# Turning the rows of every expert block on VectorE, from quarters of 64 columns

## The chip, the cores and the metric

The kernel runs on one core of a Trainium2 chip. The metric is device time in microseconds (us), the median of several runs. The engines are named as in the profile: PE is TensorE (PEld its weight loads), DVE is VectorE, ACT is ScalarE, POOL is GpSimd, and SP is SyncE, which here only issues DMAs.

## The reference

A Fourier mixing step over eight batches of 2496 rows with 256 columns is followed by a mixture of eight experts, in which each row goes to the one expert with the largest logit:

```python
X = np.fft.fft(np.fft.fft(x, axis=1), axis=2).real      # (8, 2496, 256)
x = X.reshape(19968, 256)
logits = x @ w_gate                                      # 8 experts
e = argmax(logits);  gate = softmax(logits)[e]
out = gate * (relu(x @ w1[e]) @ w2[e])                   # w1: 256 x 1024, w2: 1024 x 256
```

All of it is in float32.

## The kernel before

**Stages.** For each batch `b` there are three. `first(b)` and `regroup(b)` do one part of the transform along the rows and pass it through a DRAM tensor `Td`. `second(b)` ends the transform, finds each row's expert (`route`), and puts the row with POOL's indirect DMAs into a DRAM tensor `Xs`, which has a region for each expert. `experts` then takes blocks of 512, 256 or 128 rows of one expert from `Xs`, multiplies them with that expert's weights, and scatters the results to `out`.

**Order.** The order on each engine is written out by hand: the generators of the stages are advanced against each other by the loop over batches at line 956, with `AHEAD` (12) early steps of the next batch. Each engine works through its own instructions in program order, and so does SP's queue of DMA issues.

**Blocks.** `in_order` lists 66 blocks. Numbers 0 and 1 have 256 rows, 2 to 5 have 128, 6 to 9 have 256, 10 to 37 have 512 (10 to 12 come from batch 2). Then, in the last stage, seven blocks of 256 rows are woven with 21 blocks of 128 rows. The last seven of these 21 are computed only if the count in `tabs["cnt"]` reaches them; with the inputs here, the last three are skipped by PE, while their rows and weights are still loaded.

**Two kinds of block.** `halved(b, size)` tells them apart. Halved blocks (512 rows from batch 3 on, and the 256-row blocks of the last batch) use seven products instead of eight (`seven`, and in the last batch also `lower`), for which DVE first forms sums of the weights (`Left`, line 570) and of the rows (`right`, lines 575 to 578). All other blocks (0 to 12 and the 21 of 128 rows) use plain products: `ph` (the first layer, line 805), then `py` (the second, line 846).

**Rows of a block.** `fetch_rows` loads the rows, `turn` makes `xT` of them, with columns on the partitions and the odd columns negated. In a halved block the rows come in four DMAs of 64 columns each (L539), with the row number and gate in a fifth (L543); DVE's 32x32 transpose reads them (L588), and ACT negates one half (L590). In the other blocks one DMA brings whole rows (L534); PE transposes them against the identity into PSUM (`pt`, L596), and DVE evicts with signs (L597).

**Order of loads.** `fetch_some` issues the rows and then the weights (`w1` at L549, `w2` at L551) of a block up to two ahead, as buffers come free: `xb`, `w1` and `w2` have three each, `xT` has one. The next block is turned while the present one is at its second layer. Other transfers on SP's queue are the loads of `x` (L292), the writes and reads of `Td` (L345, L357).

Of the kernel before, what the change touches and what calls it, by code (L numbers as in the profile page):

```python
# [12 lines left out]
F32 = mybir.dt.float32  # L13
BF16 = mybir.dt.bfloat16
I32 = mybir.dt.int32
ALU = mybir.AluOpType
ACTF = mybir.ActivationFunctionType
# [3 lines left out]
B, S, D = 8, 2496, 256  # L21
# [16 lines left out]
BIG, BLK, REST = 512, 256, 128  # L38
# [8 lines left out]
def free(ap, offset, *dims):  # L47
    return bass.AP(ap.tensor, ap.offset + offset, [list(ap.ap[0])] + [list(d) for d in dims])


def bc(ap, axis, n):
    shape = list(ap.shape)
    shape.insert(axis, n)
    return ap[tuple([slice(None)] * axis + [None])].to_broadcast(shape)


def shape_consts():

    c = {}
    n1 = np.arange(NA)[:, None]  # L60
    r = np.arange(NP)
    k1 = r // 2
    im = r % 2

    def wave(n2, f):
        return f(2 * np.pi / S * ((NB * n1 + n2) * k1 % S))

    w1 = [np.where(im, wave(n2, np.sin), wave(n2, np.cos)) for n2 in range(1, NS)]
    for f in (np.cos, np.sin):
        w1 += [np.where(im, 0.0, wave(0, f)), np.where(im, wave(NS, f), 0.0)]  # L70
    c["w1"] = np.stack(w1, 1) * (k1 < NK)

    u, cs, s = np.meshgrid(np.arange(NU), np.arange(2), np.arange(NS), indexing="ij")
    u, cs, s = (v.reshape(-1, 1) for v in (u, cs, s))
    k2 = np.arange(NB)
    t = 2 * np.pi / NB * ((s + 1) * k2 % NB)
    end = np.where(cs, 1.0 - 2.0 * (k2 % 2), 1.0)
    even = np.where(s == NS - 1, end, np.where(cs, -np.sin(t), np.cos(t)))
    odd = np.where(s == NS - 1, end, np.where(cs, np.cos(t), np.sin(t)))
    own = (u == np.arange(NU)).astype(float)  # L80
    c["m2"] = np.stack([(own[:, :, None] * m[:, None, :]).reshape(GP, GP) for m in (even, odd)], 1)

    rot = np.zeros((GP, GP))
    for p in range(GP):
        if p % NS == NS - 1:
            rot[p, p] = 1.0
        elif p // NS % 2:
            rot[p, p - NS] = -1.0
        else:
            rot[p, p + NS] = 1.0  # L90
    c["rot"] = rot

    d = np.arange(H)[:, None]
    m = np.arange(D + 1)
    t = 2 * np.pi / D * (d * m % D)
    rc, rs = np.cos(t), -np.sin(t)
    rs[0] = 1.0 - 2.0 * (m % 2)
    full = np.concatenate([rc[:, :D], rs[:, :D]], 0)


    rd = np.zeros((H, 2, 2 * E + NY + 1))
    sign = 1.0 - 2.0 * (m[:NY] % 2)
    rd[:, 0, 0:NY] = sign * rc[:, 0:NY]
    rs[0] = 0.0
    rd[0, 1, 2 * E] = 1.0
    rd[:, 1, 2 * E + 1:] = sign * rs[:, 0:NY]
    c["rd"] = rd
    c["alt"] = np.broadcast_to(np.array([1.0, -1.0]), (128, 2))
    c["rt"] = full.T.reshape(2, 128, D).transpose(1, 0, 2)

    p = np.arange(128)[:, None, None, None]
    h = np.arange(2)[None, :, None, None]
    g = np.arange(HW)[None, None, :, None]
    mir = np.arange(2)
    tau = 128 * (HW * h + g) + p
    k1 = tau // NB
    k = k1 + NA * (tau % NB)
    bad = (k1 >= NK) | ((mir == 1) & ((k1 == 0) | (k1 == NK - 1)))
    row = np.where(bad, 0, np.where(mir, S - k, k))
    c["row"] = row.reshape(128, 2, NSL)  # L120
    c["good"] = 1.0 - bad.reshape(128, 2, NSL)
    c["far"] = OUT * bad.reshape(128, 2, NSL)
    c["rev"] = np.broadcast_to(E - np.arange(E), (128, E))
    c["cap"] = np.broadcast_to(CAP * np.arange(E), (128, E))
    c["sgn"] = np.where(np.arange(128) == 0, 1.0, -1.0)[:, None]
    c["lane"] = np.arange(128)[:, None]
    c["tri"] = np.triu(np.ones((128, 128)), 1)
    c["ident"] = np.eye(128)
    return {n: np.ascontiguousarray(v, dtype=np.float32) for n, v in c.items()}


# [61 lines left out]
def halved(b, size):  # L193

    return size == 512 and b > 2 or size == 256 and b == B - 1
# [22 lines left out]
def kernel(ctx: ExitStack, tc, x, w_gate, w1, w2, out):  # L218
    nc = tc.nc
    vec, act, pool = nc.vector, nc.scalar, nc.gpsimd  # L220
# [5 lines left out]
    Xs = nc.dram_tensor("Xs", (ROWS, W), F32, kind="Internal").ap()  # L226

    def const_dram(name, v):
        return nc.inline_tensor(v, name=f"c_{name}").ap()
# [17 lines left out]
    def taken(ins, b):  # L247
        ins = getattr(ins, "ins", ins)
        if b + 1 < B:
            tc.declare_no_dep(ins, group=f"xs{b + 1}", reason="a block has rows of its round's batches alone")  # L250
        tc.add_to_no_dep_group("taken", ins)
# [7 lines left out]
    pse = ctx.enter_context(tc.tile_pool(name="pse", bufs=1, space=PSUM))  # L259
# [4 lines left out]

    ctx.enter_context(tc.manual_schedule())
    consts = shape_consts()

    side = [n for n in consts if n not in ("w1", "rt")]
    packed = np.zeros((128, sum(consts[n][0].size for n in side)), np.float32)
    table = cp.tile(list(packed.shape), F32, name="table")  # L270
    con, k = {}, 0
# [9 lines left out]
    wg = cp.tile([128, 2, E], F32, name="wg")  # L281
    tri = cp.tile([128, 128], BF16, name="tri16")
    ones = cp.tile([128, 128], BF16, name="ones16")
    ident = con["ident"]
    waves = const_dram("w1", consts["w1"])

    def load(b, q):
# [239 lines left out]
    def fetch_rows(b, size, tab, i):  # L527


        n = size // 128  # L530
        row = nc.sync.value_load(tab[:, 0, i:i + 1], min_val=0, max_val=ROWS - size)
        xb = bp.tile([128, BIG // 128, W], F32, tag="xb", name="xb", bufs=3)
        if not halved(b, size):
            taken(nc.sync.dma_start(out=xb[:, 0:n].rearrange("p t c -> p (t c)"),  # L534
                                    in_=Xs[ds(row, size)].rearrange("(p t) c -> p (t c)", t=n)), b)
            return xb, xb[:, 0:n, D:]
        flat = xb[:].rearrange("p t c -> p (t c)")
        for q in range(4):
            taken(nc.sync.dma_start(  # L539
                out=flat[32 * q:32 * q + 32, 0:2 * size].rearrange("p (j e) -> p j e", e=64),  # L540
                in_=Xs[ds(row, size), 64 * q:64 * q + 64].rearrange("(j k) e -> k j e", k=32)), b)
        meta = flat[:, 4 * D:4 * D + 2 * n].rearrange("p (t c) -> p t c", c=2)
        taken(nc.sync.dma_start(out=meta, in_=Xs[ds(row, size), D:].rearrange("(t p) c -> p t c", p=128)), b)  # L543
        return flat, meta
# [27 lines left out]
    def right(xs, b11, b12, b21, b22, eng=vec):  # L572

        o = [xs[:, k] for k in range(3)]
        eng.tensor_tensor(o[0], b12, b11, op=sub)
        eng.tensor_tensor(o[1], b22, o[0], op=sub)
        eng.tensor_tensor(o[2], b21, o[1], op=sub)
        eng.tensor_tensor(b12, b22, b12, op=sub)
        return b11, b21, b22, o[2], o[0], o[1], b12

    def turn(b, size, xb):


        xT = bp.tile([128, 2, BIG], F32, tag="xT", name="xT", bufs=1)
        n = min(size // 128, 2)
        for h in range(-(-size // 256)):
            if halved(b, size):
                vec.transpose(free(xT[:], 256 * h, [32, 8], [BIG, 2], [1, 32]),  # L588
                              free(xb, 512 * h, [64, 8], [1, 2], [2, 32]))
                act.activation(xT[:, 1, 256 * h:256 * h + 256], xT[:, 1, 256 * h:256 * h + 256], ACTF.Copy, scale=-1.0)  # L590
                yield xT
                continue
            pt = pse.tile([128, 2, n, 128], F32, tag="e", name="pt")
            for c in range(2):
                for t in range(n):
                    nc.tensor.transpose(pt[:, c, t], xb[:, 2 * h + t, c:D:2], ident[:])  # L596
            vec.tensor_tensor(xT[:, :, 256 * h:256 * h + 128 * n], pt[:].rearrange("p c t k -> p c (t k)"),  # L597
                              bc(con["alt"][:], 2, 128 * n), op=ALU.mult)
            yield xT
        if halved(b, size):  # L600
            th = size // 2
            xs = bp.tile([128, 3, th], F32, tag="xs", name="xs", bufs=1)
            r = right(xs, *(xT[:, c, k * th:(k + 1) * th] for c in range(2) for k in range(2)))
            yield r
# [109 lines left out]
    def experts(todo):  # L714
# [35 lines left out]
        for k, (b, size, last, at) in enumerate(todo):  # L750
            n, m = size // 128, BIG // size
            if not k:
                while todo[0][:3] not in tabs:
                    yield 0, False
                fetch_some(0, 1)
                while b not in whole:
                    yield 0, True
                fetch_some(0)
                for _ in range(9):
                    yield 0, False  # L760
                for xT in turn(b, size, xbs[0][0]):
                    pass
# [163 lines left out]
    for _ in first(0):  # L926
# [8 lines left out]
        out=Xs[E * CAP:].rearrange("(k p) w -> p k w", k=BLK // 128), in_=bc(pad[:], 1, BLK // 128)), "xs"), 0)  # L935
# [103 lines left out]
```

## Time and profile before

| | |
|---|---|
| median of 4 runs | 1299.88 us (1297.93 to 1300.76) |
| profiled execution | 1302.36 us, of which span 1300.6 us |
| PE transposes `pt` (L596) | 98, median 281 ns, their busy time together 18.3 us |
| DVE evictions of `pt` (L597) | 37 (25 of 256 columns, mean 417 ns; 12 of 512, mean 686 ns) |
| DVE transposes (L588) | 57 of 512 columns, mean 692 ns |
| ACT negations (L590) | 57 of 256 columns, mean 415 ns |
| row loads in one DMA (L534) | 34 |
| row loads in quarters (L539) | 128, that is 32 blocks, and 32 of L543 |
| granted clock of PE, mean | 0.976 |

The profile is of one execution on the chip. Its page gives the busy time of each engine and, in 40 slices, the course of it; groups of instructions by line; and the chain of work that ended last. Timelines give each instruction with its start, duration, line, operation and tiles, and in brackets how long its engine was idle before it and what ended that. Durations of matmuls are modelled and overlap, so what an instruction costs PE is better read from the distance between starts. A DMA issue on SP shows the time of issuing, not of the transfer. Nearly all matmuls are issued by one helper and so stand under L223; they are told apart by their tiles.

### The profile page before, as it was taken

Reading aid. Unit: us, or ns where it says so; the run is one execution under the profiler, and the core shown is the slowest. Engines: PE = TensorE matmul, PEld = TensorE weight load, DVE = VectorE, ACT = ScalarE, POOL = GpSimd, SP = SyncE. Lnnn points to the kernel's source line nnn. Section 1 sums busy time; section 2 is a strip of 40 time slices with the busy share of each in tenths; the row PEclk is TensorE's granted clock in tenths of the full one; section 3 lists DMA queues with packets and bytes.
Section 4 is the critical chain, followed back from the end, with each engine's and each line's share of the span. In section 5 each row is a group of like instructions: output and inputs, shape, how many; then the busy total and the mean of one; then the engine's idle time right before and its main releaser. Section 6 shows DMA issues by size and latency. Waiting matters only on the chain.

```text
span 1300.6 us, 20743 instructions
## 1 busy us (share of the span) xinstructions
PE 1238.7 (95%) x7003; PEld 1092.1 (84%) x7003; DVE 700.6 (54%) x1772; ACT 424.1 (33%) x1059; POOL 361.5 (28%) x355
## 2 busy tenths in 40 slices
PE   6669898999999999999999999999989999999997
PEld 4558797876788888888888888888889999999996
DVE  4455434333456555666546455675468784444662
ACT  1423222331334343434334343432234332222231
POOL 0244216125014311351114411351344221111112
PEclk9859899999999999999999999999999999999998
DMA  8778697556446444583335534453345237777776
GB/s 240 251 239 281 230 325 273 200 174 229 136 134 215 162 145 154 145 263 118 113 117 181 158 104 159 125 168 106 117 126 172 90 107 287 265 279 286 276 298 234
DMA packets 134024, 249.76 MB, mean 192 GB/s; under 512 B 85065, under 2 KB 99891, under 8 KB 114332
## 3 DMA queue, kind: packets, MB, share of 16 engines
q1 hardware_dynamic: 117143, 203.33, 48.1%
q0 software_dynamic: 15888, 42.14, 9.0%
q10 hardware_dynamic: 885, 2.94, 0.7%
q8 instruction: 57, 0.93, 0.3%
q14 instruction: 51, 0.42, 0.1%
HBM read 194.97 MB, written 54.83 MB: 192 GB/s over the span
## 4 chain that ended last, share of the span: by engine, by line
PE 72%; issue 18%; POOL 3%; DMA 3%; DVE 2%; another core or an unknown queue 1%; ACT 1%; POOLq 0%; SPq 0%; ACTq 0%; DVEq 0%
PE py L223 29%; PE a L223 8%; PE c L223 7%; PE ph L223 7%; PE p L223 6%; PE d L223 4%; PE b L223 4%; PE e L223 3%; PE s L223 3%; POOL out_dram L238 3%; DMA xq<-in_x_dram 1%; DMA Td<-t 1%; PE pt L596 0%; DMA t<-Td 0%
## 5 line engine op out<-in xcount | busy, mean ns | idle before, releaser
L223 PE MATMUL py<-w_sb,hT 128*128 128x256 f32 x2016 | 457.0, 381 | 5.8 <-issue 5.8
L223 PEld LDWEIGHTS py<-w_sb,hT 128*128 128x128 f32 x2016 | 378.4, 191 | 55.3 <-issue 6.7
L238 POOL DMA_INDIRECT out_dram<-y,ro x163 | 163.2, 1001 | 731.2 <-ACT y L850 493.3
L238 POOL DMA_INDIRECT Xs<-rows,pi x160 | 163.0, 1019 | 200.0 <-ACT pi L470 82.8
L223 PE MATMUL ph<-xT,w_sb 128*128 128x128 f32 (+2 forms) x992 | 171.9, 329 | 6.5 <-DVE hT L809 5.6
L850 ACT ACTIVATE y<-py,xb 128x256 f32<-128x256 f32 x129 | 61.2, 474 | 325.8 <-PE py L223 285.3
L223 PEld LDWEIGHTS ph<-xT,w_sb 128*128 128x128 f32 x992 | 136.1, 192 | 31.1 <-issue 16.3
L223 PE MATMUL a<-xT,w_sb 128*128 128x256 f32 (+1 forms) x512 | 118.0, 357 | 3.0 <-ACT hT L644 2.0
L634 DVE TENSOR_TENSOR u<-p,b 128x512 f32<-128x512 f32 x57 | 39.2, 687 | 126.6 <-PE b L223 90.8
L809 DVE TENSOR_SCALAR hT<-ph 128x512 f32<-128x512 f32 x43 | 29.7, 691 | 138.0 <-issue 70.7
L223 PEld LDWEIGHTS a<-xT,w_sb 128*128 128x128 f32 x512 | 89.2, 190 | 15.0 <-ACT hT L644 3.6
L411 DVE COPY lg<-p 128x16 f32<-128x16 f32 x80 | 13.9, 174 | 144.9 <-ACT zs L408 139.0
L644 ACT ACTIVATE hT<-a 128x512 f32<-128x512 f32 x57 | 34.0, 597 | 156.7 <-PE a L223 120.4
L223 PE MATMUL s<-xq,w 104*112 104x256 f32 (+2 forms) x208 | 62.4, 424 | 13.0 <-DVE xq L300 11.0
L223 PEld LDWEIGHTS p<-table,t 120*128 120x128 f32 x352 | 54.6, 204 | 16.2 <-issue 5.3
L223 PE MATMUL p<-table,zz 128*128 128x145 f32 (+1 forms) x320 | 58.5, 309 | 6.6 <-issue 2.9
L223 PE MATMUL p<-table,t 120*128 120x120 f32 (+1 forms) x352 | 57.6, 290 | 7.0 <-ACT zz L382 3.3
L223 PE MATMUL c<-xT,ws 128*128 128x256 f32 (+1 forms) x256 | 59.2, 358 | 3.0 <-DVE hT L640 3.0
L811 ACT ACTIVATE hT<-ph 128x512 f32<-128x512 f32 x55 | 32.8, 597 | 83.0 <-PE ph L223 57.1
L223 PEld LDWEIGHTS s<-xq,w 104*112 104x112 f32 x208 | 39.4, 206 | 23.1 <-DVE xq L300 10.2
L223 PE MATMUL c<-xs,ws 128*128 128x256 f32 (+1 forms) x256 | 58.8, 357 | 0.0
L223 PE MATMUL d<-xT,w_sb 128*128 128x256 f32 (+1 forms) x256 | 58.7, 356 | 0.0
(148 smaller groups left out, 1761.5 us busy)
## 6 DMA issues: line engine op xcount, KB each, us to landing
w_sb<-in_moe_w_dram SPq DMA_DIRECT2D x132, 1024.0 KB
xq<-in_x_dram SPq DMA_DIRECT2D x24, 896.0 KB
xb<-Xs SPq DMA_DIRECT2D x100, 128.0 KB
Td<-t SPq DMA_DIRECT2D x18, 448.0 KB
t<-Td SPq DMA_DIRECT2D x8, 768.0 KB
t<-Td SPq DMA_DIRECT2D x8, 640.0 KB
xb<-Xs SPq DMA_DIRECT2D x25, 129.0 KB
Td<-t ACTq DMA_DIRECT2D x6, 448.0 KB
```

Source lines behind the costliest of these rows:

```text
L223: nc.tensor.matmul(o, lhsT=lhsT, rhs=rhs, start=start, stop=stop, **kw)
L238: return unordered(pool.indirect_dma_start(out=dst, out_offset=bass.IndirectOffsetOnAxis(ap=idx, axis=0), in_=rows, in_offset=None, bounds ...
L411: vec.tensor_copy(lg[:, k:k + 2], p3[:, NY:NY + 2 * E].rearrange("p (m e) -> p m e", m=2))
L634: vec.tensor_tensor(u2[:], p1[:], b[:], op=add)
L644: act.activation(h11, a[:], ACTF.Relu)
L809: vec.tensor_scalar(o, ph[:], 0.0, None, op0=ALU.max)
L811: act.activation(o, ph[:], ACTF.Relu)
L850: act.activation(y[:], py[:], ACTF.Copy, scale=meta[:, i, 1:2])
```

## The change

All blocks take the way of the halved ones. `fetch_rows` always issues four quarters and the fifth DMA, and `turn` always uses DVE's transpose and ACT's negation, for 128 rows with half as many columns. The constants for the old way, the identity and the alternating signs, leave the packed table, which is 130 columns narrower. Products, blocks, buffers and the order of the steps stay.

```diff
@@ shape_consts
-    c["alt"] = np.broadcast_to(np.array([1.0, -1.0]), (128, 2))
...
-    c["ident"] = np.eye(128)
@@ fetch_rows
         xb = bp.tile([128, BIG // 128, W], F32, tag="xb", name="xb", bufs=3)
-        if not halved(b, size):
-            taken(nc.sync.dma_start(out=xb[:, 0:n].rearrange("p t c -> p (t c)"),
-                                    in_=Xs[ds(row, size)].rearrange("(p t) c -> p (t c)", t=n)), b)
-            return xb, xb[:, 0:n, D:]
         flat = xb[:].rearrange("p t c -> p (t c)")
         for q in range(4):
             taken(nc.sync.dma_start(
@@ turn
-        n = min(size // 128, 2)
+        n = min(size, 256)
         for h in range(-(-size // 256)):
-            if halved(b, size):
-                vec.transpose(free(xT[:], 256 * h, [32, 8], [BIG, 2], [1, 32]),
-                              free(xb, 512 * h, [64, 8], [1, 2], [2, 32]))
-                act.activation(xT[:, 1, 256 * h:256 * h + 256], xT[:, 1, 256 * h:256 * h + 256], ACTF.Copy, scale=-1.0)
-                yield xT
-                continue
-            pt = pse.tile([128, 2, n, 128], F32, tag="e", name="pt")
-            for c in range(2):
-                for t in range(n):
-                    nc.tensor.transpose(pt[:, c, t], xb[:, 2 * h + t, c:D:2], ident[:])
-            vec.tensor_tensor(xT[:, :, 256 * h:256 * h + 128 * n], pt[:].rearrange("p c t k -> p c (t k)"),
-                              bc(con["alt"][:], 2, 128 * n), op=ALU.mult)
+            vec.transpose(free(xT[:], 256 * h, [32, n // 32], [BIG, 2], [1, 32]),
+                          free(xb, 512 * h, [64, n // 32], [1, 2], [2, 32]))
+            odd = xT[:, 1, 256 * h:256 * h + n]
+            act.activation(odd, odd, ACTF.Copy, scale=-1.0)
             yield xT
```

More of the change, by code (lines that the diff above doesn't have):

```diff
@@ L283 @@
     ones = cp.tile([128, 128], BF16, name="ones16")
-    ident = con["ident"]
     waves = const_dram("w1", consts["w1"])
```

## The prediction

> **What bounds the kernel now.** I read the page's first two parts, then stretches, then the timelines of TensorE (PE), SyncE (SP) and VectorE (DVE) in the last stage, and last the list of waits.
>
> ```profile
> span 1300.6 us, 20743 instructions
> PE 1238.7 (95%) x7003; PEld 1092.1 (84%) x7003; DVE 700.6 (54%) x1772; ACT 424.1 (33%) x1059; POOL 361.5 (28%) x355
> ```
> ```profile
> 207.00:214.00 7.00, 3.23 (x15) 2.50 (x15) 2.43 (x10) 0.63 (x5) 4.27 (x5) 1.00 0.96 273
> ...
> 1081.00:1287.00 206.00, 206.00 (x1577) 198.54 (x1576) 102.68 (x226) 52.19 (x103) 32.14 (x31) 1.00 0.76 278
> ```
>
> The second fence is from the table of stretches (length, busy time of PE, PEld, DVE, ACT, POOL, PE clock, DMA share, GB/s). From 142 us on PE hardly rests: it is busy 64.69 of the 65 us up to 207 and 128.80 of the 131 from 214 to 345, and in the last stage all 206 of 206 us, with DVE at half. The exceptions are 207 to 214, where DMA is at 0.96 and PE works 3.23 of 7 us, and the time before 142. So an instruction taken from PE after 142 us shortens the run, unless what PE waits for next is late. The candidates are seen in one cycle of the last stage:
>
> ```profile
> 1088.81 3.73 PE L223 MATMUL ph<-xT,w_sb 128*128 128x128 f32 x32
> 1092.38 0.40 PE L596 MATMUL pt<-table,xb 128*128 128x128 f32 x2
> 1092.62 3.62 PE L223 MATMUL py<-w_sb,hT 128*128 128x256 f32 x16
> 1096.08 3.73 PE L223 MATMUL ph<-xT,w_sb 128*128 128x128 f32 x32
> 1099.65 3.62 PE L223 MATMUL py<-w_sb,hT 128*128 128x256 f32 x16
> 1103.10 1.05 PE L223 MATMUL a<-xT,w_sb 128*128 128x128 f32 x8
> ```
> ```profile
> 1082.50 0.34 SPq L534 DMA_DIRECT2D xb<-Xs  x1
> 1083.97 0.03 SPq L549 DMA_DIRECT2D w_sb<-in_moe_w_dram  x1
> ...
> 1089.51 1.91 SPq L539 DMA_DIRECT2D xb<-Xs  x4
> 1091.62 0.40 SPq L543 DMA_DIRECT2D xb<-Xs  x1
> 1092.87 0.36 SPq L549 DMA_DIRECT2D w_sb<-in_moe_w_dram  x1
> ```
> ```profile
> 1098.57 0.69 DVE L570 TENSOR_TENSOR ws<-w_sb 128x512 f32<-128x512 f32 x1 [4.85 <-DMA w_sb<-in_moe_w_dram]
> ...
> 1101.11 0.70 DVE L588 STREAM_TRANSPOSE xT<-xb 128x512 f32<-128x512 f32 x1
> ```
>
> A 128-row block is ph then py; the transposes of its follower (pt) stand between. At 1103.10 a 256-row block begins. Its rows and weights were issued by SP at 1089.51 to 1093.5, its w1 was there at 1098.57, when DVE had already waited 4.85 us, and then come four additions, the transpose, ACT's negation, and PE.
>
> **What is removed.** 98 transposes on PE (row L596, x98). Their price is the step they put between starts, not their duration: ph to py takes 1092.62-1088.81 = 3.81 us with two of them and 1099.65-1096.08 = 3.57 without, so 0.24 for two, 0.12 each; 98 x 0.12 = 11.8 us. Where they lie: 56 in blocks 0 to 12 (six of 256 rows with 4, four of 128 with 2, three of 512 with 8), 42 before the 21 last small blocks. Blocks 0, 1 and 2 are turned before 142 us, where PE waits anyway (busy 12.39 us from 120 to 140): 10 count nothing. Two pairs at the very end (1288 and 1292 us) lie beside skipped blocks: 4 count nothing. On the path are 84, so 10.1 us. Fourteen of them lie between 142 and 207 us, ahead of the hole at 207 to 214; if that hole is set by DMA it swallows their 1.7 us. I take -8.4, with -10.1 as the other end.
>
> [...]
>
> **What takes their place.** On DVE 37 evictions of pt (L597: 686 ns for 512 columns, 417 for 256) become 37 transposes: 692 ns for 512 (L588); 256 columns are not in the trace, between 0.35 (half) and 0.69, and I take 0.42, as the 128x256 additions of L575 have. DVE's sum stays. ACT gets 37 negations (L590, 415 ns for 256 columns; for 128, between 0.2 and 0.42, I take 0.36 as L675's 128x128 form has), some 14 us on an engine that is 33% busy. Is the new chain DVE then ACT in time? Between small blocks DVE ends L809 0.7 us into py, so xT is ready about 1.6 us into a py of 3.46: cover 1.8 us. If ACT or DVE were late by more, PE would lose the excess. DVE's queue now waits for the rows where PE's did; behind it stand L809 and ro. PE waited for rows once, 2.63 us at the very end. So 0, up to +1 for the first block, whose turn gets ACT's step (90.54 to 91.28 us is now DVE's alone).
>
> **The rows.** 34 loads (one issue, 0.34 us) become 34 x 5. SP needs 1.51 us from rows to weights with one issue (1096.78 to 1098.29) and 3.36 with five (1089.51 to 1092.87): each of these blocks' weights, and all else queued on SP behind them (Td writes L345, x loads L292, regroups L357), are issued 1.85 us later; and 2.9 later where the five are themselves slowed (1123.80 to 1128.23). Bytes stay; packets become 256 B. From 1126 to 1129 us, when little else moved:
>
> ```profile
> q1 hardware_dynamic: 976, 0.18, 37.3%
> ```
>
> 37.3% of 16 engines x 3 us / 976 = 18 ns a packet. A 128-row block has 512 of 256 B and 128 small ones, at most 640 x 18 = 11.5 engine-us, 0.7 us of the 16 engines, less what its 128 long packets take now; in the last stage the share is 0.76 of a 7 us period, so there is room on average, but w1 of the 256-row block is not an average.
>
> Margin there: transpose start + 0.70 + 0.42 + 0.04 of hops against PE's entry gives 0.8, 0.6, 0.6, 0.9, 0.6 and 1.2 us at 1103, 1137, 1172, 1206, 1233 and 1260 us. The change eats 0.24 of each (the faster block between trigger and entry), and of the 1.85 us by which the previous block's weights slip some part reaches w1. From 1092 to 1095 DMA is not full, so much of it is absorbed: between 0 and 1.85, I take 0.7. Stall per entry: 0.7+0.24-0.8, about 0.15, some +1.0 over six; ends 0 and 6 x 1.3 = +8.
>
> Early, SP's thirteen loads cost 13 x 1.85 = 24 us of SP, nearly all beside SP's own waits (it waits 91.9 and 88.9 us for ACT at L345). Exposed can be loads 3 and 9 (121.8 and 207.3 us), issued when DMA is full and PE about to starve: 0 to 2 x 1.85 = +3.7; I take +1.5, between them.
>
> The end: the last block's rows are issued at 1288.17, and PE waits for them until 1292.14. With five issues the last leaves 2.1 us later, but PE no longer stands before it: ends -0.5 and +2, I take +0.9. The constant table loses 130 columns (66 of 494 KB): at the 240 GB/s of the first slices 0.3 us of a DMA that is 0.93 busy; -0.2.
>
> **Sum.** -8.4 +1.0 +1.5 +0.9 -0.2 = -5.2 us. The profiled execution took 1302.36 (span 1300.6), 2.5 above the median 1299.88 of four; the difference goes on the median: 1294.7.
>
> **Rivals.**
> 1. Weights come too late, and the kernel is slower. Mechanism: one place, SP's queue; rows take 2.5 us instead of 0.34 and weights leave 1.85 later. It decides once more than about 0.5 us of that reaches w1's landing. For it: w1 is what DVE waits for at six entries (29.4 us in total), and DMA is at 0.9 in the small-block stretches. Against it: SP's and DMA's pauses (1112 to 1117 us DMA moves nothing). Price: the far ends together, +8 in the tail, +3.7 in the two early holes, +2 at the end, against -8.4 and -0.2: +5, so 1305.
> 2. No change: PE's time comes back as waits at the entries and in the holes. Half of the tail's 38 x 0.12 = 4.6 us and all of the early 3.8 lost, the end paid: -2.3+0.9-0.2 = -1.6, so 1298.3. For it: DVE already waits up to 5.1 us for weights. Against it: every entry has margin, and early blocks 4 to 12 find PE without a pause.
> 3. Nothing is late at all: -10.1, -0.2 and the end at -0.5 make -10.8, so 1289.1.
>
> That PE would not be relieved is excluded: the calls are gone from the code, and 512-row blocks already run this way (L588 x57).
>
> **How the numbers follow.** The forecast (with rival 3 at its lower end) gets 0.58, rival 2 0.16, rival 1 0.26, high because two waits of 5.8 and 3.8 us (PE for py and for L809) show how dear one late transfer is there. A measurement tells some 0.2%, 2.6 us, from no change, and the chances of faster, same and slower are these three. Range 1289.5 to 1304.0: the lower end is all of PE's time, the upper takes in most of rival 1. The likeliest case's own range is 1289.5 to 1297.3.
>
> **What the changed profile would show.** Row L596 gone; L588 and L590 at x94, L539 at x264. A small block from ph to ph 7.03 us everywhere instead of 7.27; if it stays, PE was not the limit. Weights issued 3.3 us after the first row quarter. At the six entries PE idle below 0.3 us; over 1 us means rival 1. Holes near 130 and 210 us no longer than now. The last rows' issues at L539 and L543 2.5 us long. I am wrong if PE's idle time between 142 and 1290 us grows by more than 5 us.

## The result, and the profile after

The changed kernel took 1296.65 us (median; 1289.37 to 1305.63), the kernel before, run beside it, 1300.64: a ratio of 0.9965, 95% interval 0.9956 to 0.9975, that is -4.5 us (-5.7 to -3.2). The forecast was -5.2 us and 1294.7. The page of the profiled execution after:

```profile
span 1296.5 us, 21062 instructions
PE 1231.5 (95%) x6905; PEld 1082.9 (84%) x6905; DVE 701.9 (54%) x1772; ACT 436.0 (34%) x1096; POOL 361.7 (28%) x355
```

PE has 98 matmuls less (7003 to 6905) and 7.2 us less work, ACT 37 instructions and 12 us more. The new shapes, from the groups of instructions with shapes kept apart (total, then mean ns of one):

```profile
L580 DVE STREAM_TRANSPOSE xT<-xb 128x256 f32<-128x256 f32 x25 | 10.9, 436 | 4.8 <-DMA xb<-Xs 4.8
L583 ACT ACTIVATE xT<-xT 128x128 f32<-128x128 f32 x25 | 7.7, 310 | 65.3 <-DVE ro L753 38.3 <-DVE xT L580 16.9 <-DVE hT L794 10.2
```

436 and 310 ns, where the prediction took 420 and 360. (In the kernel after, L221 is the matmul helper, L580/L583 the turn, L532/L536 the row loads, L542 the load of w1, L563 Left's additions.) The table of stretches (length, busy PE, PEld, DVE, ACT, POOL, PE clock, DMA share, GB/s), for the hole and for the last stage:

```profile
207.00:214.00 7.00, 4.85 (x11) 3.87 (x12) 3.60 (x13) 0.86 (x4) 3.07 (x4) 0.54 1.00 304
...
1081.00:1281.00 200.00, 197.50 (x1493) 188.47 (x1493) 100.68 (x219) 55.37 (x117) 29.00 (x29) 1.00 0.80 280
```

Two things differ from before. In the stretch from 207 to 214 us, into which the hole falls in whole (before) or in part (after), PE's clock is 0.54, not 1.00. And PE no longer fills the last stage: 2.5 us are idle where there was none. The timelines of PE and SP over the small block ahead of the first 256-row entry:

```profile
1088.72 3.73 PE L221 MATMUL ph<-xT,w_sb 128*128 128x128 f32 x32
1092.29 3.62 PE L221 MATMUL py<-w_sb,hT 128*128 128x256 f32 x16
1095.75 0.46 PE L221 MATMUL a<-xT,w_sb 128*128 128x128 f32 x2
```
```profile
1089.42 1.96 SPq L532 DMA_DIRECT2D xb<-Xs  x4
1091.57 0.35 SPq L536 DMA_DIRECT2D xb<-Xs  x1
1092.76 0.35 SPq L542 DMA_DIRECT2D w_sb<-in_moe_w_dram  x1
```

ph to py is 3.57 us, as predicted, and the block lasts 7.03 instead of 7.27. Weights leave 3.34 us after the first quarter. So the mechanism does what was said. Yet the lead over before does not grow over the last stage: at the first 256-row entries (1067.94 before, 1061.22 after) it was 6.7 us, at the first skipped block (1287.57 and 1280.97) 6.6. Of the 38 x 0.12 = 4.6 us of relief that the prediction counted there, nearly all must have gone, most likely at the entries. The fourth of the six, PE and then DVE:

```profile
1199.50 1.16 PE L221 MATMUL a<-xT,w_sb 128*128 128x128 f32 x8 [0.48 <-DVE xT L580]
...
1205.71 1.16 PE L221 MATMUL c<-xT,ws 128*128 128x128 f32 x8 [0.58 <-DVE hT L625]
```
```profile
1196.20 0.69 DVE L563 TENSOR_TENSOR ws<-w_sb 128x512 f32<-128x512 f32 x1 [6.48 <-DMA w_sb<-in_moe_w_dram]
...
1198.74 0.70 DVE L580 STREAM_TRANSPOSE xT<-xb 128x512 f32<-128x512 f32 x1
...
1204.97 0.69 DVE L625 TENSOR_TENSOR hT<-u,c 128x512 f32<-128x512 f32 x1
```

PE stands twice: at the entry, as foreseen, and six products later, for an addition that is late because DVE's whole queue behind w1 is late. And the end is longer: from the first skipped block to the end of the span 15.5 us, before 13.0:

```profile
1281.58 1.95 SPq L532 DMA_DIRECT2D xb<-Xs  x4
1283.72 0.35 SPq L536 DMA_DIRECT2D xb<-Xs  x1
```
```profile
1288.47 0.45 DVE L580 STREAM_TRANSPOSE xT<-xb 128x256 f32<-128x256 f32 x1 [4.76 <-DMA xb<-Xs]
```

The last rows are there 6.9 us after the first of their issues, before 4.0 (1288.17 to 1292.14).

### The profile page after: what moved, and what is told of

Read it like the earlier page. It is cut to its first block, busy times and chain, and to the rows that moved or that the text cites. A ratio compares the mean times of both kernels' runs of the same rounds, so it can differ in the third digit from the quotient of the medians.

```text
span 1296.5 us, 21062 instructions
## 1 busy us (share of the span) xinstructions
PE 1231.5 (95%) x6905; PEld 1082.9 (84%) x6905; DVE 701.9 (54%) x1772; ACT 436.0 (34%) x1096; POOL 361.7 (28%) x355
## 5 line engine op out<-in xcount | busy, mean ns | idle before, releaser
L221 PE MATMUL py<-w_sb,hT 128*128 128x256 f32 x2016 | 457.5, 381 | 4.5 <-DVE hT L794 4.5
L221 PEld LDWEIGHTS py<-w_sb,hT 128*128 128x128 f32 x2016 | 379.5, 191 | 55.2 <-DVE hT L794 4.9
L221 PE MATMUL ph<-xT,w_sb 128*128 128x128 f32 (+2 forms) x992 | 175.7, 333 | 8.5 <-DVE hT L794 4.5
L221 PEld LDWEIGHTS ph<-xT,w_sb 128*128 128x128 f32 x992 | 138.6, 195 | 34.3 <-issue 19.1
L221 PE MATMUL a<-xT,w_sb 128*128 128x256 f32 (+1 forms) x512 | 118.1, 358 | 1.9 <-ACT hT L629 1.4
L794 DVE TENSOR_SCALAR hT<-ph 128x512 f32<-128x512 f32 x43 | 29.7, 691 | 139.9 <-issue 78.2
L221 PEld LDWEIGHTS a<-xT,w_sb 128*128 128x128 f32 x512 | 89.0, 190 | 14.2 <-ACT hT L629 2.6
L583 ACT ACTIVATE xT<-xT 128x256 f32<-128x256 f32 (+1 forms) x94 | 36.4, 387 | 135.9 <-DVE xT L580 78.2
L221 PE MATMUL s<-xq,w 104*112 104x256 f32 (+2 forms) x208 | 62.8, 427 | 13.2 <-DVE xq L297 8.5
L221 PEld LDWEIGHTS p<-table,t 120*128 120x128 f32 x352 | 55.7, 208 | 16.0 <-issue 9.2
L221 PE MATMUL p<-table,t 120*128 120x120 f32 (+1 forms) x352 | 58.7, 294 | 6.7 <-issue 4.8
L221 PE MATMUL c<-xT,ws 128*128 128x256 f32 (+1 forms) x256 | 59.6, 360 | 5.0 <-DVE hT L625 3.4
L221 PE MATMUL p<-table,zz 128*128 128x145 f32 (+1 forms) x320 | 58.0, 307 | 4.1 <-issue 2.3
L580 DVE STREAM_TRANSPOSE xT<-xb 128x512 f32<-128x512 f32 (+1 forms) x94 | 58.2, 625 | 4.8 <-DMA xb<-Xs 4.8
L221 PEld LDWEIGHTS s<-xq,w 104*112 104x112 f32 x208 | 39.6, 207 | 23.5 <-DVE xq L297 9.9
```

The source lines that it names most:

```text
L221: nc.tensor.matmul(o, lhsT=lhsT, rhs=rhs, start=start, stop=stop, **kw)
L580: vec.transpose(free(xT[:], 256 * h, [32, n // 32], [BIG, 2], [1, 32]), free(xb, 512 * h, [64, n // 32], [1, 2], [2, 32]))
L583: act.activation(odd, odd, ACTF.Copy, scale=-1.0)
L794: vec.tensor_scalar(o, ph[:], 0.0, None, op0=ALU.max)
```

## Experiments

Two theories stand against each other: the prediction's sum (PE's relief is kept but for 1.0 us at the entries, 1.5 early, 0.9 at the end), and the reading above (the last stage gives its relief back, and the end costs 2.5). Twelve kernels were run in three groups, each beside the kernel before on its chip: e1 to e4 on one chip, e5 to e12 on another. In the first group before took 1276.7 us, in the others 1299.8 and 1298.8: in the profiles of the first the long early waits near 130 us are nearly absent. All differences below are ratio minus one, times before's median, with the 95% interval.

### One part of the change alone

```diff
+def turned_by_vector(b, size):
+    return halved(b, size) or b == B - 1      # e1; e2: or b < B - 1
...
-        if not halved(b, size):
+        if not turned_by_vector(b, size):
...
-            if halved(b, size):
+            if turned_by_vector(b, size):
```

> Only the 21 small blocks of the last batch come in quarters and are turned by VectorE; the thirteen blocks of the first rounds stay with one load and TensorE. Theory of the prediction's sum: 38 transposes x 0.12 = -4.6, stalls at entries +1.0, the end +0.9, so -2.7 us against the kernel before. Rival, from the trace of after (the lead over before was 6.7 us at 1068 us and 6.6 at the first skipped block, and the end was 2.5 us longer): the tail's relief is used up by waits at the 256-row blocks and the end costs 2.5, so +2 us.

> Only the thirteen blocks of the first rounds (0 to 12) come in quarters and are turned by VectorE; the last batch is as before. Prediction's sum: 46 transposes x 0.12 = -5.5, of which the hole at 207 us swallows 1.7, exposed loads +1.5, so -2.3 us against before. Rival from the trace of after: all of the change's gain is made here, -6 us or more.

The tail alone: **-0.6 us** (-1.9 to +0.6). The early blocks alone: **-2.3** (-3.6 to -0.9), as the sum had it. The tail's -2.7 is outside its interval, and so is the rival's +2. That all of the gain is made early (-6) is refuted too.

### Relief and price taken apart

```diff
 # e3: one load of long packets, then DVE's transpose and ACT's negation
-        if not turned_by_vector(b, size):         # in fetch_rows
+        if not halved(b, size):
 # e4: quarter loads, then PE's transposes
-            if turned_by_vector(b, size):         # in turn
+            if halved(b, size):
...
-  nc.tensor.transpose(pt[:, c, t], xb[:, 2 * h + t, c:D:2], ident[:])
+  nc.tensor.transpose(pt[:, c, t], xb[:, 256 * (2 * h + t) + c:256 * (2 * h + t) + D:2], ident[:])
```

> The relief without its price: every block is turned by VectorE and negated by ScalarE, but blocks of rounds 0 to 2 and the small blocks of the last batch still come in one load of long packets (their rows are then wrongly arranged, so values differ; amounts of work are the same). Prediction's sum: -8.4 us with nothing of the prices (a late-turn chain would show as less); if the turn by VectorE and ScalarE is itself late at entries, only -4.

> The price without the relief: every block comes in four quarter loads and one of the two last columns, but blocks of rounds 0 to 2 and the small ones of the last batch are still transposed by TensorE (wrongly arranged values, same amounts of work). Prediction's sum: entries +1.0, loads 3 and 9 +1.5, the end +0.9 (or +2), so +3.4 us against before. Rival: the loads cost what the trace of after seems to show, some 4 us at entries and 2.5 at the end, so +6 us or more. If e3 and e4 add to the change's -4.5, relief and price are independent.

Relief alone: **-8.2** (-10.0 to -6.3), where the sum has -8.4. Price alone: **+9.6** (+7.9 to +11.1), nearly three times the 3.4. They add to +1.4, and the two parts on the same chip to -2.9, so they are not independent. The loads cost more where PE itself waits for the rows: in e4's list of waits PE stands 12.6 us for xb, at the first block and at the end; the old parts of e1 and e2 have 7.1 and 2.3 there.

Where the early loads cost is seen in the stretch of the longest wait near 210 us and the 7 us behind it, in e1 (early part old) and then e2 (early part new):

```profile
211.15:212.05 0.90, 0.00 (x1) 0.00 (x0) 0.21 (x1) 0.60 (x1) 0.77 (x1) 1.00 1.02 401
212.05:219.05 7.00, 7.00 (x38) 6.28 (x39) 1.38 (x2) 0.89 (x3) 1.18 (x2) 1.00 0.85 346
```
```profile
208.23:210.69 2.46, 0.00 (x0) 0.00 (x0) 0.20 (x1) 0.60 (x1) 2.03 (x2) 0.92 1.09 407
210.69:217.69 7.00, 7.00 (x23) 6.10 (x24) 1.31 (x2) 1.30 (x4) 0.98 (x1) 0.54 0.88 359
```

PE waits for t from Td. The SP timelines of the two show why; e1, then e2 (edited kernels have other line numbers: here L539 is the load in one DMA, L544 the quarters, L362 the loads of t):

```profile
194.43 0.37 SPq L539 DMA_DIRECT2D xb<-Xs  x1
...
196.95 3.23 SPq L362 DMA_DIRECT2D t<-Td  x2
```
```profile
192.29 3.02 SPq L544 DMA_DIRECT2D xb<-Xs  x4
...
198.30 2.15 SPq L362 DMA_DIRECT2D t<-Td  x2
```

From the rows of block 9 to the loads of t SP takes 2.5 us with one issue and 6.0 with five. The wait is 1.6 us longer, about what the prediction gave loads 3 and 9 together, and then the clock runs at 0.54 for 7 us, which by an estimate doubles the cost or more. The estimate takes PE's work as in proportion to the clock (the eight products of ph behind the wait take 3.43 us in e2, from their first start to the next instruction's, and 1.74 in e1): 7 us at 0.54 are 3.2 us of work lost, at the 0.76 that e4 shows (wait of 2.40) 1.7. This second price was nowhere in the sum. That PE comes to the wait earlier explains little of it: e3, with the relief and one load, waits 1.31 us there, e4, with five issues and no relief, 2.40.

All this holds for the chip of the first group. In the profiles of before and of the change PE stands near 210 us for something else. Before (DVE, then PE), and after (PE):

```profile
212.39 0.69 DVE L809 TENSOR_SCALAR hT<-ph 128x512 f32<-128x512 f32 x1 [4.47 <-remote]
```
```profile
213.14 1.99 PE L223 MATMUL ph<-xT,w_sb 128*128 128x256 f32 x8 [3.77 <-DVE hT L809]
```
```profile
209.15 3.78 PE L221 MATMUL ph<-xT,w_sb 128*128 128x256 f32 x8 [4.52 <-DVE hT L794]
```

PE waits for DVE to empty ph, and DVE has waited for something that the profile does not name. The first product that reads t comes at 227.53 (after: 225.63), without a wait. What block 9's loads do to this wait is not shown.

### The change on another chip, and two of its prices mended

```diff
 # e6: in the last batch w1's load ahead of the rows, w2's behind them
+  if b == B - 1 and len(got) <= n and (b, size, last) in tabs and b in whole:
+      part = fetch_w1(tabs[b, size, last], at)
+      xbs.append(fetch_rows(b, size, tabs[b, size, last], at))
+      got.append(fetch_w2(*part))
+      continue
 # e7: old way for block 9;  e8: e6's edit, and old for block 9 and the last three
+  return not (b == 1 and at == 3)
+  return not (b == 1 and at == 3 or b == B - 1 and size == REST and at >= SURE + 4)
```

> The change itself, unaltered, beside the next three on the same chip. If the last batch (-0.6) and the first rounds (-2.3) add, -2.9 us against before; the forecast had -5.2. It is the base for the three that follow.

> The change, and in the last batch a block's first weights are issued ahead of its rows, its second weights behind them. Theory: PE loses its relief there at the six entries because w1 lands late and VectorE's work behind it is late; issued some 5 us earlier, VectorE's wait for w1 (33 us in six) goes to under 5 and PE keeps its relief: -3.5 us against the change. Rival: the transfers themselves are the limit there (share 0.8), or the rows now come late: within 1 us of the change.

> The change, but the rows of block 9 alone (256 rows, fetched at about 192 us) come in one load and are transposed by TensorE. Theory: its five issues stand on SyncE ahead of the two loads of t from Td, for which TensorE waits at about 208 us; with one issue that wait is 0.9 instead of 2.5 us, TensorE's granted clock stays at 1.00 behind it instead of 0.50 for some 6 us; four transposes come back (+0.5). Together -1.6 -3 +0.5 = -4 us against the change. Rival: the wait has another cause (transfers saturated), and the kernel is 0.5 us slower.

> The change with both edits of the two runs before, and the last three blocks (their matmuls are skipped with these data) old as well: one load, TensorE. If all three theories hold: -3.5 -4 and -1.5 for the end = -9 us against the change, some -12 against before. If the rivals hold: within 2 us of the change.

The change: **-4.4** (-6.9 to -1.8). With w1 first: **-7.8** (-10.4 to -5.2), so -3.4 against the change, as the theory said. The two intervals overlap, but the traces place it. The entry in e6 that answers to the one above, PE and DVE:

```profile
1202.22 1.05 PE L221 MATMUL a<-xT,w_sb 128*128 128x128 f32 x8
...
1207.58 1.06 PE L221 MATMUL c<-xT,ws 128*128 128x128 f32 x8
```
```profile
1195.66 0.69 DVE L566 TENSOR_TENSOR ws<-w_sb 128x512 f32<-128x512 f32 x1 [2.58 <-DMA w_sb<-in_moe_w_dram]
```

No wait of PE is left, DVE starts 6.56 us ahead of the entry instead of 3.30, and DVE's wait for w1 is 6.6 us in all instead of 33.0 (30.7 in e5). The table gives each execution's gain on the profile of before, from the last entry ahead of the small blocks (1067.94 us there) to the first skipped block:

| kernel | gain in the last stage, us |
|---|---|
| relief only (e3); loads only (e4) | 4.2; -0.7 |
| the change, in three profiles (the first one, e5; e7) | -0.1, 2.1, 2.1 |
| tail only (e1); last blocks old (e10) | 0.4; 1.5 |
| w1 first (e6, e8, e11) | 4.1, 3.7, 3.9 |
| last batch old (e2, e9, e12) | 0.7, 0.0, 0.1 |

The kernels of the first chip (e1 to e4) are to be read against e2: nothing is changed there in the last stage, and it gains 0.7, most of it in a wait of the first entry that is 0.56 us shorter than in before. So the relief is worth 3.4 us on that chip, and on the other some 4 us are kept with w1 first; the change as it stands loses 2 to 4 of them at the entries. That w1's place in the queue is the cause is shown by the edit: it brings them back where all rows come in quarters, and moves nothing in this stage where the small blocks come in one load (e9). Each entry of the table is one execution.

Block 9 old: **-4.0** (-6.2 to -1.8), not better than the change. The theory of e7 wanted -8.4 against before, which is outside the interval: on this chip undoing that one load bought nothing that can be measured. Its trace has the shorter wait (1.21 us at 211 us, clock 1.00 behind it), but then one of 2.57 us, which ends at 226. And e8, where block 9 is old as well, waits 3.84 us, with a clock of 0.76 behind it. The theory had taken the first chip's wait, for t, for this chip's, which is the other one above.

The three edits: **-12.5** (-15.1 to -10.0), 8 us under the change: the best version found.

### Controls

```diff
 # e10: the change, last three blocks old;  e11: with e6's edit as well
+  return not (b == B - 1 and size == REST and at >= SURE + 4)
```

> Control: the kernel before, with the last batch's first weights issued ahead of the rows as in the run before. Theory: before the change TensorE stood at no entry for w1, so there is nothing to win: within 1.5 us of before (the change with the same edit was 7.2 us under before). Rival: the edit is worth 3 us whatever the rows' way, and the change only looks better with it: -3 us.

> The change, but the last three blocks (their matmuls are skipped with these data) come in one load and are transposed by TensorE as before. Theory: the end of the change, 2.5 us longer by the traces from the first skipped block to the span's end, is given back: -2 us against the change, -6.4 against before. Rival: the end's last transfer is late for another reason: no gain.

> Two of the three edits: first weights first in the last batch, and the last three blocks old; block 9 stays quartered. Theory: block 9's way was worth nothing (0.9 us slower than the change, within its interval), so this is as fast as the three edits, -12 us against before. Rival: block 9 matters once the rest is mended: 3 us slower than the three edits, -9.

> The thirteen early blocks quartered, the last batch as before, once more, for a chip on which before takes 1300 and not 1277 us. If the early part behaves as in the first look, -2.3 us; if the long waits near 130 and 208 us on such a chip swallow the early relief, within 1 us of before, and the change's -4.4 is made in the last batch.

(By the ratios e7 was 0.4 us slower than the change; the 0.9 in e11's text is the difference of the medians, and there e7 was the faster.)

Before with w1 first: **-2.9** (-5.6 to -0.1), a miss, nearer the rival. By the times alone the edit is worth as much before (-2.9) as on the change (-3.4). It is the profiles that tell the two apart: in the last stage the edit moves nothing here (0.0 in the table), so the theory holds there. In its profile 3.0 us are saved behind it, at the end: 10.05 us from the first skipped block to the end instead of 13.0.

Last blocks old: **-6.4** (-8.4 to -4.2), as expected to the tenth; the intervals of it and of the change overlap. The end is 12.5 us long in its profile, and 15.5 and 15.4 in two of the change. Its SP and PE at the end:

```profile
1275.04 0.33 SPq L539 DMA_DIRECT2D xb<-Xs  x1
```
```profile
1277.76 0.48 PE L603 MATMUL pt<-table,xb 128*128 128x128 f32 x2 [1.38 <-issue]
```

Rows are turned 2.7 us after their issue begins, not 6.9.

Two edits: **-10.8** (-13.5 to -7.9), between what theory (-12) and rival (-9) wanted. Whether block 9's way matters beside the other two is not settled.

Early blocks alone again: **-1.9** (-4.0 to 0.0), as on the first chip.

## Why the prediction held

**PE's step, 0.12 us a transpose, 98 of them: right.** e3 has -8.2 for the -8.4; its interval reaches to -10.0, so it does not decide whether the hole swallows the 14 transposes ahead of it (on that chip the wait there is 1.31 us with the relief and 0.90 in e1). In a stretch without holes, from block 2's ph to block 6's py, the lead grows by 1.65 us in the first profile of the change (145.90 and 142.15 to 192.99 and 187.59), the same in e5, e10, e11 and e12, and by 0.0 in e9, which is old there: 14 x 0.12 = 1.68. By the median duration in before, 281 ns, these 14 would have made 3.9 us; the runs show the step. With rows in quarters of 64 columns blocks of 32x32 are enough for the turn (the patterns of `turn` in the diff), and e3's -8.2 says that VectorE's way is worth 8 us as long as its rows come no dearer.

**DVE and ACT in cover, 0: right** for the small blocks (7.03 us each).

**Entries, +1.0: mis-sized; 2 to 4 us.** The mechanism was right, w1's landing at six places, and the slip was no more than the guess of 0.7: from w1's issue to DVE's first use took 5.24 us on the mean of the six before, 5.92 in the first profile of the change (up to 7.1) and 5.49 in e5. The issue itself stands as far ahead of the entry as before (9.7 us on the mean of the six in both profiles); it is the weights of the block in front that leave 2 to 3 us later. That this is what slows w1 is argued from the times; that its place in the queue decides is shown by e6. It was the margin that was wrong. The prediction took 0.6 to 1.2 us, by the entry alone. The binding place is six products on, where PE's c waits for hT: before, that addition was done at 1107.34 + 0.69 = 1108.03 and PE began at 1108.46, 0.4 us. The turn stands in the middle of DVE's queue, not at its end. With 0.4 for 0.8, the sum's own line gives 0.7 + 0.24 - 0.4 = 0.5 each, +3.2 over six.

**Loads 3 and 9, +1.5: right in size on the first chip, incomplete in the price; open elsewhere.** 1.6 us more at load 9 on the first chip, nothing that shows at load 3 (the wait near 120 us is 1.07 us in e1 and in e2, and neither stands near 130), and behind load 9 the clock. How much it costs on the other chips the runs do not tell: there five profiles with block 9 and all else quartered, and the first one, lie between 1.8 us worse and 2.8 better than before from 190 to 376 us, e9, old in that part, is 1.6 worse, and e7 and e8, with block 9 old, are 4.9 and 1.0 better. The wait itself, which on those chips is for DVE, grew from 3.77 to 4.52 us in the first profile and is 3.01 in e5.

**The end, +0.9: mis-sized; +2.5 in the profiles, -1.9 when mended (e10).** The bound of +2 counted the issues alone. What lies behind was left out: DVE can begin only 5.3 us after the last quarter's issue (1283.17), with DMA at 0.82 or more all that time, and then the transpose, ro and ACT (L583) stand in a row before the last y.

**The sum.** -8.4 with +3 for the entries, +1.5, +2.5 and -0.2 for the shorter table (which no run takes apart) would be -1.6, or less with the clock; -4.4 and -4.5 were measured. The parts alone make -0.6 and -2.3 or -1.9, so -2.5 to -2.9. About 1.7 us lie between that and the whole; the intervals reach over it, and no run says whether it is more than chance. The forecast's -5.2 is therefore nearer, by luck, than its terms deserved: two were too small.

**The rivals.** Rival 2 (half the tail's relief comes back as waits) is what the last stage does; it failed in the early blocks, which keep about 2 us. Rival 1's mechanism, w1 behind SP's queue, is the true one, at a quarter to a half of its +8. Rival 3's place without lateness is reached by e8, on the far side of its -10.8, but not by the change alone: w1 first is worth 2.9 us in before too. Of the marks, PE idle at an entry under 0.3 us was missed once (0.48), and the hole near 210 us was longer in the first profile. The sign of being wrong, PE's idle time from 142 to 1290 us growing by more than 5, came true as it was written: 12.8 us became 20.5. Only 2.0 of that lie ahead of 1280 us (12.3 to 14.3); the rest is PE standing at the skipped blocks, which the changed profile reaches 6.6 us earlier, so that the mark, set by the clock and not by the work, measured something else.

## What to carry to other kernels

Work taken off the bounding engine pays only until the next landing that was just in time, so margins are to be read along the whole queue behind that landing, not at the first consumer alone (here 0.4 us at c, where 0.8 was read at the entry). Splitting a load into many issues moves everything queued behind it on the same issuer (the loads of t came 6.0 us behind block 9's rows with five issues, 2.5 with one); put what is needed soonest first in that queue (w1 first: -7.8 us for the change's -4.4), and leave the split out where nothing covers it (the last blocks old: -6.4). A wait of the matrix engine can cost more than its length: behind waits of 2.40 to 4.52 us near 210 us its clock was 0.54 to 0.79 over the next 7 us in ten profiles of eleven.

## What the runs showed of the hardware

**The clock behind a wait.** The longest idle time of PE near 210 us and its granted clock in the 7 us that follow, over fourteen profiles: after 0.90, 1.21 and 1.31 us it stayed at 1.00; after 2.40 to 4.52 us it was 0.54 to 0.79 in ten profiles and 1.00 in one, the profile of before (3.77 us), which so hid the price. Shorter waits can be followed by the same. In the profile of the change PE stands 1.89 us for ACT near 228 us, and then:

```profile
228.12 0.78 PE L221 MATMUL p<-table,t 120*128 120x120 f32 x2 [1.89 <-ACT t L372]
```
```profile
228.00:230.00 2.00, 1.89 (x6) 1.62 (x7) 0.00 (x0) 0.42 (x2) 0.00 (x0) 0.50 0.13 45
```

The clock is 0.50 over these 2 us; in before it is 1.00 (230 to 232 us) behind a wait of the same length (1.89 us) at the same place. Near 210 us too 0.50 is what 2-us stretches show, in the change from 208 to 214 us and in e2 from 212 to 216. The length of the wait alone does not settle it: of four waits of 3.75 to 3.84 us (e6, before, e10, e8) three have 0.76 to 0.79 behind them and one, that of before, 1.00. What does is not shown.

**The same kernel on two chips.** Before took 1276.7 us on one and 1298.8 to 1300.6 in all other measurements. The wait near 130 us (5.78 us before, 3.9 to 8.1 in the other profiles from slower chips) is absent on the faster one (from 90 to 140 us PE is busy 48.41 of the 50 us in e1, whose code is the same up to there, and 41.30 in before). Why is open; in before DVE, just ahead of the end of that wait, had stood 9.90 us for something that the profile does not name, as near 210 us.

**Profiles against medians.** Between 939 and 970 us the profile of before stands some 3 us longer than that of the change (30.4 us for the block, 27.5); e9, old there too, is as short as the change (27.2), e5, the change again, is not (29.7), and at 1068 us e9 leads by 6.35 us with nothing changed up to there. The 6.7 us that the changed profile led by at that point were therefore no measure of the change; only a stretch in which the lead grows by the same amount in every profile is.
